# Splitting the negated softmax maxima before their transpose, and noise on a planner's due times

## The chip, the cores and the metric

The kernel runs on one core of one Trainium2 chip. The core has TensorE (matmuls), VectorE, ScalarE and GpSimd (elementwise work), and SyncE, whose queue (SP) issues all data transfers of this kernel. The metric is the device time of one execution in microseconds (us); of several runs the median is given.

## What is computed

The reference is a transformer block of two parts, each behind a modulated layer norm and added to its input through a gate. The first part is causal attention in four segments of 512 tokens with a compressive memory; the second mixes tokens with a two-layer MLP.

```python
for s in range(4):                         # 32 heads of 32 channels
    logits = einsum("bhqd,bhkd->bhqk", qs, ks) * scale + mask
    a_dot = einsum("bhqk,bhkd->bhqd", softmax(logits), vs)
    a_mem = (phi(qs) @ M) / (phi(qs) @ z + 1e-6)
    o = g * a_mem + (1 - g) * a_dot
    M, z = M + phi(ks).T @ vs, z + phi(ks).sum(l)
x = x + ga * (o @ wo)
u = gelu(einsum("bsd,sf->bdf", layernorm(h2), w1) + b1)
x = x + gb * (einsum("bdf,fs->bds", u, w2) + b2).transpose()
```

What matters here is the softmax: the maximum of each query's logits is subtracted before the exponential.

## The kernel before, in words

**Number format.** The large matmuls run on float32 values rounded to a shorter format (fp32r), so each operand is split into a high part and the remainder, a low part, and three products are summed (high x high, high x low, low x high). `split` (lines 103 to 110) does this with a ScalarE copy and a VectorE subtraction.

**Attention.** The 32 items of work are (pass, group of four heads, segment): 8 groups of heads x 4 segments, in two passes of two segments. An item is called t, its heads h = 0..3, and n = 4t + h counts heads over all. For each item `project` computes keys and values (L176) and queries (L184) on TensorE, and `stack` (L342 to L344) sends the high and low parts of queries and keys of each head into a stacked tile sk of 98 partitions: 96 for the three products, and two more, 96 and 97, that hold 1 on the key side and the negated maximum, high and low part, on the query side. One matmul over 98 partitions thus gives logits with the maximum already subtracted.

**Maxima.** `maxima(t, h)` multiplies queries by keys over the first 96 partitions (L448), one block of 128 queries at a time, into the banks sx, sy and sz of PSUM (two banks under the tag s1), and VectorE adds the mask and reduces each block to a maximum per query (L449), written to a column of mx. A pair of heads shares one mx tile of 128 queries x 8 columns (2 heads x 4 blocks). After the second head of a pair: TensorE transposes mx to 8 x 128 (L455) into the PSUM bank with the tag ms, ScalarE copies it with the sign turned and rounded (nt0, L457), VectorE computes the remainder (nt1, L458), and SP issues four transfers (L462) of four rows of nt, 2 KB each, into partition 96 or 97 of sk, in the order first head high, first head low, second head high, second head low. There are 64 such pairs.

**Scores and values.** `scores(t, h)` follows three heads later (LEADS): logits from all 98 partitions (L472, L475, L478, L479), exponentials on ScalarE (L473, L476, L480), the causal edge and the split of the result on GpSimd and ScalarE (L483, L485, L487), and then `values` (L501) multiplies by the values. L472 is the first instruction that needs the negated maxima in sk.

**After attention.** An output projection (L691) with layer norms follows, then the MLP as block products (L790) with results added by VectorE (L797). These stages stream large weight transfers through SP.

**What sets the order.** The program is first written down in the order of the loops; then `set_order` plans it. `Order.forward` is a list scheduler: it gives every instruction a cost (`cost`, `transfer`), walks time forward, and on each engine picks, among the ready instructions, the one with the smallest key. `Order.backward` does the same from the end and returns a due time for each, which is the next key. This is done three times (PASSES), and the order of the last forward pass is imposed on each engine's queue, SP's too. Every queue runs in order: an instruction that waits holds up all behind it. In the plan a transfer of at most 4096 bytes takes 580 ns to issue, and lands 130 ns after the transfers issued before it.

Of the kernel before, what the change touches and what calls it, by code (L numbers as in the profile page):

```python
# [4 lines left out]

# [4 lines left out]
F32 = mybir.dt.float32  # L10
F32R = mybir.dt.float32r
F16 = mybir.dt.float16
BF16 = mybir.dt.bfloat16
AF = mybir.ActivationFunctionType
ALU = mybir.AluOpType
# [5 lines left out]
P = 128  # L21
# [17 lines left out]
HB = 3  # L39
WO0 = 65  # L40
WOS = 6
TILES = (3, 4, 5, 6, 0, 1, 8, 2, 9, 10, 11, 7, 12, 13, 14, 15)


def attention_and_mlp(ctx, tc, x, wq, wkv, wo, beta, w1, b1, w2, b2, c, wm_a, wm_b, out):
    nc = tc.nc
    V, A, G, T, SY = nc.vector, nc.scalar, nc.gpsimd, nc.tensor, nc.sync
# [17 lines left out]
    a = par.__enter__()  # L65
# [11 lines left out]
    def bank(tag, bufs, name):  # L77
        return psum.tile([P, 512], F32, tag=tag, bufs=bufs, name=name)

    A.preload_act_table_set("natural_log_exp_and_others")  # L80
    ident = top.tile([P, P], F32, name="ident")
# [182 lines left out]
    for i in range(2):  # L264
        ps = bank("pj", 2, f"scps{i}")
# [47 lines left out]
    b = late.__enter__()  # L313
# [124 lines left out]
    def maxima(t, h):  # L438
        d = st[t]
        if h % 2 == 0:  # L440
            d["mx"] = b.tile([P, 2, 4], F32, tag="mx", bufs=2, name=f"mx{t}_{h}")
        mx = d["mx"]
        q, k = d["sk", h][0:96, 0], d["sk", h][0:96, 1]
        x = bank("s1", 2, f"sx_{t}_{h}")
        y = bank("s1", 2, f"sy_{t}_{h}")
        z = bank("s1", 2, f"sz_{t}_{h}")
        for i, o in ((0, x[:, 0:128]), (2, x[:, 128:512]), (1, y[:, 0:256]), (3, z)):
            T.matmul(o, q[:, 128 * i:128 * i + 128], k[:, 0:128 * i + 128], start=True, stop=True)  # L448
            V.tensor_tensor_reduce(  # L449
                o, o, mask[:, 384 - 128 * i:], 1.0, -3.0e38, op0=ALU.add, op1=ALU.max,  # L450
                accum_out=mx[:, h % 2, i:i + 1])
        if h % 2 == 0:
            return
        ps = bank("ms", 1, f"nmps{t}_{h}")
        T.transpose(ps[0:8, 0:128], mx.rearrange("p a b -> p (a b)"), ident)  # L455
        nt = [b.tile([8, P], F32R, tag=f"nt{i}", bufs=2, name=f"nt{i}_{t}_{h}") for i in range(2)]
        A.activation(nt[0], ps[0:8, 0:128], AF.Copy, scale=-1.0)  # L457
        V.scalar_tensor_tensor(nt[1], ps[0:8, 0:128], -1.0, nt[0].bitcast(F32), op0=ALU.mult, op1=ALU.subtract)  # L458
        for hh in range(2):
            sk = d["sk", h - 1 + hh]  # L460
            for part in range(2):
                SY.dma_start(sk[96 + part:97 + part, 0].bitcast(F32).rearrange("p (b n) -> p b n", n=128),  # L462
                             nt[part][4 * hh:4 * hh + 4].bitcast(F32))

    def scores(t, h):
        d = st[t]
# [126 lines left out]
    for g in range(2, NG):  # L593
        n = 8 * g - 13
# [5 lines left out]
    for j in range(32):  # L600
        n = ML0 + MLS * j
        later(n, lambda j=j: mod_fetch(j), n + 2, lambda r, j=j: mod_late(j, r))
    plan(WO0 - 3, lambda: spread(gaw, 0))
    for i in range(8):
        n = WO0 + WOS * i
        later(n, lambda i=i: wo_fetch(i), n + 2, lambda r, i=i: wo_split(i, r))

    for n in range(-LEADS, 4 * NI + VL):
# [4 lines left out]
        if 0 <= m + 4 < 4 * NI:  # L613
            t = (m + 4) // 4
# [8 lines left out]
        if 4 * NI - 5 <= m < 4 * NI + 3:  # L623
            i = m - 4 * NI + 5
# [107 lines left out]

    for tt in TILES:
        rest = out_proj(tt)
# [132 lines left out]
    for u, (ph, g) in enumerate(units):  # L867
# [59 lines left out]
        t = tp.tile([P, 3, 512], F32, tag="tu", bufs=1, name=f"tu{g}")  # L927
# [26 lines left out]
                             acc[g][:, 2 * m:2 * m + 2].rearrange("p a n -> p (a n)"))  # L954


ISSUED, LANDED, READ = 900.0, 500.0, 500.0
BACKLOG, BULK = 1000.0, 200000
LATE = 1000.0
LATEB = 3000.0  # L960
HOLD = 1000.0
EARLY = 60000.0
LINK0, SPREAD, QUICK = 2000.0, 45000.0, 1.0
EAGER = 200.0
WD, WA = 250.0, 100.0
SOON = 30000.0
WAIT = {"DVE": WD, "Activation": WA}
STAY = 3000.0
SLACK = 1.06
DMA_SPREAD = 7000.0  # L970
DONE = 11.0
LINK = 1
COLD = 20000.0
SPARE = 40000.0
MINT = 5
AVOID = 0.0
FREED = 60.0
WAKE = {"PE": 150.0, "DVE": 23.0, "Activation": 23.0, "Pool": 70.0, "SP": 60.0}
RIGHT = ("top", "st2", "late2", "b3", "wr", "s1", "cw")
PASSES = 3  # L980


def space(t):
    return str(t.space)
# [51 lines left out]
def tiled(x):  # L1036
    return [a for a in (*x.outs, *x.ins) if hasattr(a, "bass_ap")]


def cost(x):  # L1040


    e, op = x.engine.name, x.opcode
    n = max((math.prod(s[1] for s in list(v.ap)[1:]) for v in (*x.outs, *x.ins) if hasattr(v, "ap")), default=1)
    aps = tiled(x)
    if e == "PE":
        m = x.ins[0]
        c, dt = math.prod(s[1] for s in list(m.ap)[1:]), m.dtype
        if dt == F32:
            held = 223 if c in (132, 1) else 111  # L1050
        elif dt == F32R:
            held = max(63, c / 2.25 + (20 if aps[0].bass_ap.tensor.name[0] == "a" else 4))
        else:
            held = c / 2.26
        return held, held + 170, False
    if op == "DMACopy":
        return transfer(x)[0], 0, False
    psum = any(hasattr(v, "bass_ap") and space(v.bass_ap.tensor) == "PSUM" for v in x.ins)
    ins = sum(hasattr(v, "bass_ap") for v in x.ins)
    shared = False  # L1060
    if e == "DVE":
        if op == "ISA":
            return 135 + 1.05 * n, 220 + 1.05 * n, False
        if op == "TensorTensor":
            d = 145 + 1.055 * n
        elif op == "TensorScalarPtr":
            d = 155 if n < 64 else 120 + 1.1 * n
        else:
            d = {"TensorCopy": 820, "BNStats": 680, "TensorReduce": 554}.get(op, 195)
        shared = n >= 256 and ins > 1 and not psum  # L1070
    elif e == "Activation":
        if op == "TensorCopy":
            d = 185 + 0.76 * n if psum else 200 + 0.825 * n
        else:
            d = 250 + 0.85 * n + (150 if ins > 2 else 0) if n > 8 else 250
    elif op == "TensorTensor":
        d = {512: 1500, 640: 1454, 1024: 2900}.get(n, 520)
    elif op == "TensorScalarAffineSelect":
        d = 180 + n
    else:  # L1080
        d = 110 + 0.95 * n
    d *= SLACK
    return d - 85, d, shared


class Order:
# [192 lines left out]
    def forward(self, key):  # L1279
# [21 lines left out]
        def add(i):  # L1301
# [10 lines left out]
            x = self.X[i]  # L1312
            more = HOLD if self.side(x) and ready[i] > EARLY else 0.0
            if self.spread(i):
# [12 lines left out]
        while len(seq) < n:  # L1327
            t, e, i = self.pick(free, heap, future, key)
            soon = WAIT.get(e, 0.0) if t < SOON else 0.0
            if soon and future[e] and future[e][0][0] <= t + soon:  # L1330
                near = [(key[j], r, j) for r, j in future[e] if r <= t + soon]
                k, r, j = min(near)
                if k < key[i] - EAGER and r < t + self.C[i][0]:
                    heapq.heappush(heap[e], (key[i], i))
# [49 lines left out]
            for s in strong[i]:  # L1384
                done(s, t if E[s] == e == "PE" else fin[i] + WAKE.get(E[s], 30.0))
            for s in weak[i]:
                done(s, t + 1)
            for tl in tiles_of[i]:
                left[tl] -= 1
                freed[tl] = max(freed[tl], fin[i] + FREED)  # L1390
                if not left[tl]:
# [21 lines left out]
    def backward(self, start, fin, seq):  # L1413
# [9 lines left out]
        for old, i in self.took:  # L1423
            for u in self.users[old]:
                if u != i:
                    before[i][u] = max(fin[u] - start[u] + FREED, before[i].get(u, 0))
        for i in range(n):
            for d in before[i]:
                open_[d] += 1
        due = [max(s, d - SPARE) for s, d in zip(start, self.due(before, start, fin, seq))]  # L1430
        free, heap, future = defaultdict(float), defaultdict(list), defaultdict(list)
# [4 lines left out]
        for _ in range(n):  # L1436
            t, e, i = self.pick(free, heap, future, key)
            z = max(t, ready[i])
            late[i], free[e] = -z, z + (max(transfer(self.X[i])[:2]) if LINK and e == "SP" else self.C[i][0])
            for d, lag in before[i].items():  # L1440
# [4 lines left out]
        return late  # L1445


def set_order(nc, tc):

    o = Order(list(nc.cur_bb.bb.instructions))  # L1450
    start, fin, seq = o.forward(range(len(o.X)))
    for _ in range(PASSES):
        start, fin, seq = o.forward(o.backward(start, fin, seq))
    prev = {}
    behind = mybir.DependencyInfo(mybir.DependencyClass.NoSync, mybir.DependencyReason.DATA)
    for i in seq:
        x, e = o.X[i], o.E[i]
        if e in WAKE:
            if e in prev:
                tc.add_manual_dep(x, prev[e], behind, reason="order")  # L1460
            prev[e] = x.name
    return max(fin)
# [38 lines left out]
```

## Time and profile before

| what | us |
|---|---|
| median of three runs | 2209.34 |
| runs | 2207.14, 2209.35, 2209.34 |
| the profiled execution's own time | 2212.39 |
| its span, first to last instruction | 2210.6 |
| TensorE busy | 2170.2 |
| VectorE busy | 1728.2 |
| ScalarE busy | 1099.7 |
| GpSimd busy | 715.1 |

In the profile PE is TensorE's matmuls, PEld its weight loads, DVE VectorE, ACT ScalarE, POOL GpSimd, SP the queue of SyncE, and SPq and the like the queues that issue. L462 is line 462 of the kernel. `sk<-nt` is an operation that writes tile sk from tile nt. Idle time of an engine is put down to what ended it. A busy TensorE isn't one at its peak, since matmuls are pipelined: the idle time counts as lost, the busy time says little. PEclk is the clock that was granted to TensorE, as a share of full speed.

### The profile page before, as it was taken

To read this page: it belongs to the slowest core of one execution; us is meant where nothing else is said; L and a number is where in the kernel's file an instruction comes from. 1 tells how busy PE (TensorE), PEld (TensorE's weight loads), DVE (VectorE), ACT (ScalarE), POOL (GpSimd) and SP (SyncE) were. 2 spreads that over 40 slices of the span, in tenths; PEclk is the share of its full clock that TensorE was granted. 3 is DMA by queue.
4 is the path that set the end of the run, shared out by engine and by line. 5 is a ranking of instruction groups with operands and counts; after the bars stand their busy time and mean duration, and the time that the engine had idled before them with its cause. 6 is when DMAs were issued, how large, how long until landed. Compare 5 with 4: busy or idle time off the path is not lost.

```text
span 2210.6 us, 38316 instructions
## 1 busy us (share of the span) xinstructions
PE 2170.2 (98%) x13760; PEld 1882.7 (85%) x13760; DVE 1728.2 (78%) x3817; ACT 1099.7 (50%) x2008; POOL 715.1 (32%) x829
## 2 busy tenths in 40 slices
PE   8999999999999999999999999999999999999999
PEld 7899998989898999978878888888888888888887
DVE  8787776867787755678997555898889787878787
ACT  6687787566665766562434333533334242424232
POOL 1476676476776756570001000043221000000000
PEclk9999999999999999999999999999999999999999
DMA  9667666796677643674467555775549241414144
GB/s 384 193 192 215 174 213 190 240 292 201 194 227 237 184 131 101 173 243 164 138 238 274 193 200 191 276 272 202 200 175 335 92 157 58 147 54 148 58 124 152
DMA packets 174769, 421.74 MB, mean 191 GB/s; under 512 B 17356, under 2 KB 71668, under 8 KB 165620
## 3 DMA queue, kind: packets, MB, share of 16 engines
q1 hardware_dynamic: 174580, 419.30, 58.2%
q8 instruction: 109, 1.79, 0.3%
q14 instruction: 80, 0.66, 0.1%
HBM read 242.00 MB, written 126.37 MB: 167 GB/s over the span
## 4 chain that ended last, share of the span: by engine, by line
PE 85%; DVE 5%; DMA 4%; ACT 2%; POOL 2%; issue 1%; SPq 0%; DVEq 0%; ACTq 0%; POOLq 0%
PE mx L790 47%; PE nps L176 12%; PE po L691 6%; PE qps L184 6%; PE pv L501 4%; POOL ph L487 1%; PE a L472 1%; PE sx L448 1%; PE sz L448 1%; PE up L430 1%; PE rd L420 1%; DVE wm L286 1%; PE a L475 1%; DMA rawv<-in_wkv_dram 1%; DMA sk<-nt 1%
## 5 line engine op out<-in xcount | busy, mean ns | idle before, releaser
L790 PE MATMUL mx<-bU,sp 128*128 128x512 f32 x2352 | 533.7, 389 | 0.8 <-DVE bU L110 0.8
L790 PEld LDWEIGHTS mx<-bU,sp 128*128 128x128 f32 x2352 | 441.3, 188 | 93.0 <-DVE bU L110 1.2
L107 ACT CAST sp<-wr 128x384 fp32r<-128x384 f32 (+2 forms) x408 | 218.4, 545 | 468.8 <-PE mx L790 382.9
L176 PE MATMUL nps<-wv,h 128*128 128x256 f32 x3072 | 440.3, 283 | 1.9 <-DVE r L373 1.4
L790 PE MATMUL mx<-bA,sp 128*128 128x512 f32 x1764 | 433.5, 390 | 1.7 <-ACT sp L107 0.9
L487 POOL TENSOR_TENSOR ph<-p,ph 128x640 f16<-128x640 f32 x256 | 385.6, 1523 | 104.6 <-ACT ph L485 104.2
L176 PEld LDWEIGHTS nps<-wv,h 128*128 128x128 f32 x3072 | 402.0, 189 | 8.4 <-DVE r L373 1.6
L790 PEld LDWEIGHTS mx<-bA,sp 128*128 128x128 f32 x1764 | 330.6, 188 | 72.9 <-ACT sp L107 1.9
L110 DVE TENSOR_TENSOR sp<-wr,sp 128x384 fp32r<-128x384 f32 (+2 forms) x408 | 257.3, 639 | 60.4 <-ACT sp L107 60.0
L797 DVE TENSOR_TENSOR ac<-mx,ac 128x512 f32<-128x512 f32 x280 | 190.5, 687 | 94.8 <-PE mx L790 93.9
L184 PE MATMUL qps<-h,wq 128*128 128x512 f32 x768 | 199.6, 403 | 0.0
L485 ACT CAST ph<-p 128x1280 f16<-128x1280 f32 x128 | 161.3, 1260 | 48.3 <-POOL p L483 47.9
L691 PE MATMUL po<-wo,ots 128*128 128x512 f32 x768 | 181.7, 391 | 0.5 <-DVE x L694 0.3
L691 PEld LDWEIGHTS po<-wo,ots 128*128 128x128 f32 x768 | 143.1, 188 | 29.9 <-DVE x L694 0.9
L184 PEld LDWEIGHTS qps<-h,wq 128*128 128x128 f32 x768 | 141.3, 191 | 29.1 <-issue 0.3
L790 PE MATMUL mx<-bB,sp 128*128 128x512 f32 x588 | 165.7, 389 | 0.0
L483 POOL TENSOR_SCALAR_AFFINE_SELECT p<-p 128x256 f32<-128x256 f32 x256 | 118.0, 471 | 134.5 <-ACT p L476 95.7
L449 DVE CUSTOM_DVE_ANT_0 sx<-sx,mask 128x128 f32<-128x128 f32 (+1 forms) x256 | 110.6, 433 | 62.6 <-PE sx L448 60.4
L662 POOL TENSOR_TENSOR tu<-cc 128x512 f32<-128x512 f32 x14 | 20.0, 1426 | 399.2 <-DVE cc L926 372.2
L790 PEld LDWEIGHTS mx<-bB,sp 128*128 128x128 f32 x588 | 110.4, 188 | 22.9
L501 PE MATMUL pv<-vp,ph 128*128 128x97 bf16 (+1 forms) x2560 | 118.3, 201 | 0.1
L501 PEld LDWEIGHTS <-ph 128*128 128x128 f16 x2560 | 108.1, 98 | 5.8 <-issue 1.2
(184 smaller groups left out, 3246.4 us busy)
## 6 DMA issues: line engine op xcount, KB each, us to landing
sk<-sg SPq DMA_DIRECT2D x384, 128.0 KB
wr<-in_w_dram SPq DMA_DIRECT2D x28, 1024.0 KB
wr<-in_w_dram SPq DMA_DIRECT2D x32, 768.0 KB
bstu<-ucd SPq DMA_DIRECT2D x28, 768.0 KB
wv<-wsp SPq DMA_DIRECT2D x36, 512.0 KB
wsp<-wv SPq DMA_DIRECT2D x32, 512.0 KB
rawm<-in_wm_b_dram SPq DMA_DIRECT2D x32, 512.0 KB
pcd<-cc SPq DMA_DIRECT2D x14, 1024.0 KB
```

The source lines that it names most:

```text
L107: A.copy(hi, src)
L110: lo_eng.tensor_tensor(lo, src, hi.bitcast(F32), op=ALU.subtract)
L176: T.matmul(ps[:, aa], h[:, j, 128 * tt:128 * tt + 128], wt[:, i, o:o + 256], start=(n == 0), stop=(n >= 6 * NK - 2), skip_group_check=True)
L184: T.matmul(ps, wt[:, i, o:o + 128], h[:, j], start=(k + n == 0), stop=(3 * k + n == 3 * NK - 1))
L449: V.tensor_tensor_reduce(o, o, mask[:, 384 - 128 * i:], 1.0, -3.0e38, op0=ALU.add, op1=ALU.max, accum_out=mx[:, h % 2, i:i + 1])
L483: G.affine_select(w, w, pattern=[[0, 2], [1, 128]], compare_op=ALU.is_ge, fill=0.0, base=0, channel_multiplier=-1)
L485: A.copy(ph[:, 0], p32)
L487: G.tensor_tensor(ph[:, 1, c], p32[:, c], ph[:, 0, c], op=ALU.subtract)
L501: T.matmul(pv[:, i, 0:w], ph[:, part, o:o + 128], d["vp"][:, j, h, 0:w], start=(n == 0), stop=(n == 19), skip_group_check=True)
L691: T.matmul(ps, os_[:, i, P * ct:P * ct + P], wop[ct, nh][:, j], start=(n == 0), stop=(n == 3 * NK - 1))
L790: T.matmul(ps, ops[q][:, i, P * k:P * k + P], b[:, j], start=(m == 0 and first), stop=(m == 3 * nk - 1), skip_group_check=True)
L797: V.tensor_tensor(d, ps, d, op=ALU.add)
```

## The change

Three things are changed. First, VectorE negates the maxima and takes their high and low parts before the transpose, on the 128 x 8 tile, into a new tile mm of 128 x 16 with four buffers (MM); its columns are ordered by head, then part, then block. TensorE transposes 16 columns at once, ScalarE copies 16 x 128 to one tile nt (three buffers in place of two of each part), and one transfer for each head moves eight rows of nt, 4 KB, into partitions 96 and 97 of sk.

Second, after the last pass of the planner a further forward pass is run, with the same due times plus noise: `nudged` adds a Gaussian number to the due time of every instruction whose planned start lies in a stretch. There are 25 entries of (seed, from, to, width), times in ns of the plan.

Third, many constants of the planner can be read from the environment; their values are as before.

```diff
@@ maxima, after the second head of a pair
+        mm = b.tile([P, 2, 2, 4], F32R, tag="mm", bufs=MM, name=f"mm{t}_{h}")
+        V.tensor_scalar(mm[:, :, 0], mx, -1.0, None, op0=ALU.mult)
+        V.scalar_tensor_tensor(mm[:, :, 1], mx, -1.0, mm[:, :, 0].bitcast(F32), op0=ALU.mult, op1=ALU.subtract)
         ps = bank("ms", 1, f"nmps{t}_{h}")
-        T.transpose(ps[0:8, 0:128], mx.rearrange("p a b -> p (a b)"), ident)
-        nt = [b.tile([8, P], F32R, tag=f"nt{i}", bufs=2, name=f"nt{i}_{t}_{h}") for i in range(2)]
-        A.activation(nt[0], ps[0:8, 0:128], AF.Copy, scale=-1.0)
-        V.scalar_tensor_tensor(nt[1], ps[0:8, 0:128], -1.0, nt[0].bitcast(F32), op0=ALU.mult, op1=ALU.subtract)
+        T.transpose(ps[0:16, 0:128], mm.rearrange("p a c b -> p (a c b)").bitcast(F32), ident)
+        nt = b.tile([16, P], F32R, tag="nt", bufs=3, name=f"nt{t}_{h}")
+        A.copy(nt, ps[0:16, 0:128])
         for hh in range(2):
             sk = d["sk", h - 1 + hh]
-            for part in range(2):
-                SY.dma_start(sk[96 + part:97 + part, 0].bitcast(F32).rearrange("p (b n) -> p b n", n=128),
-                             nt[part][4 * hh:4 * hh + 4].bitcast(F32))
+            SY.dma_start(sk[96:98, 0].bitcast(F32).rearrange("p (b n) -> p b n", n=128),
+                         nt[8 * hh:8 * hh + 8].bitcast(F32))
...
+NUDGES = (
+    (839485, 482000.0, 512000.0, 300.0),
+    (324712, 922000.0, 1022000.0, 100.0),
+    (608137, 521000.0, 551000.0, 300.0),
+    (337605, 0.0, 30000.0, 800.0),
+    (965332, 417000.0, 1517000.0, 100.0),
...
+    (347681, 480000.0, 510000.0, 800.0),
...
+    (684163, 133000.0, 163000.0, 300.0),
...
+)
...
+def nudged(o, key, start, nudges):
+    key = list(key)
+    for seed, lo, hi, width in nudges:
+        rnd = random.Random(seed)
+        for i in range(len(key)):
+            if lo <= start[i] < hi:
+                key[i] += rnd.gauss(0.0, width)
+    return key
...
     start, fin, seq = o.forward(range(len(o.X)))
     for _ in range(PASSES):
-        start, fin, seq = o.forward(o.backward(start, fin, seq))
+        key = o.backward(start, fin, seq)
+        start, fin, seq = o.forward(key)
+    start, fin, seq = o.forward(nudged(o, key, start, NUDGES))
```

Of the 25 stretches, four begin before 200 us, two between 200 and 300, and the other 19 lie from 370 us on, all but one of them ending by 1022 us.

More of the change, by code (lines that the diff above doesn't have):

```diff
@@ L2 @@
 import math
+import random
 from collections import defaultdict
@@ L41 @@
 WOS = 6
+MM = 4
 TILES = (3, 4, 5, 6, 0, 1, 8, 2, 9, 10, 11, 7, 12, 13, 14, 15)
@@ L954, in attention_and_mlp @@
                              acc[g][:, 2 * m:2 * m + 2].rearrange("p a n -> p (a n)"))
+import os
+EV = lambda n, d: type(d)(os.environ.get(n, d))
 ISSUED, LANDED, READ = 900.0, 500.0, 500.0
-BACKLOG, BULK = 1000.0, 200000
-LATE = 1000.0
+BACKLOG, BULK = EV("BACKLOG", 1000.0), 200000
+LATE = EV("LATE", 1000.0)
 LATEB = 3000.0
 HOLD = 1000.0
[L962 to L966, printed above, removed]
+EARLY = EV("EARLY", 60000.0)
+LINK0, SPREAD, QUICK = EV("LINK0", 2000.0), EV("SPREAD", 45000.0), 1.0
+EAGER = EV("EAGER", 200.0)
+WD, WA = EV("WD", 250.0), EV("WA", 100.0)
+SOON = EV("SOON", 30000.0)
 WAIT = {"DVE": WD, "Activation": WA}
-STAY = 3000.0
+STAY = EV("STAY", 3000.0)
 SLACK = 1.06
 DMA_SPREAD = 7000.0
-DONE = 11.0
-LINK = 1
+DONE = EV("DONE", 11.0)
+LINK = EV("LINK", 1)
 COLD = 20000.0
-SPARE = 40000.0
+SPARE = EV("SPARE", 40000.0)
 MINT = 5
 AVOID = 0.0
-FREED = 60.0
-WAKE = {"PE": 150.0, "DVE": 23.0, "Activation": 23.0, "Pool": 70.0, "SP": 60.0}
+FREED = EV("FREED", 60.0)
+WAKE = {"PE": EV("WP", 150.0), "DVE": 23.0, "Activation": 23.0, "Pool": 70.0, "SP": EV("WS", 60.0)}
 RIGHT = ("top", "st2", "late2", "b3", "wr", "s1", "cw")
-PASSES = 3
+NUDGES = (
[4 more added lines that the diff above has]
+    (965332, 417000.0, 1517000.0, 100.0),
+    (781737, 833000.0, 933000.0, 100.0),
+    (929601, 783000.0, 813000.0, 800.0),
+    (705508, 676000.0, 706000.0, 300.0),
+    (882468, 168000.0, 268000.0, 100.0),
+    (566630, 374000.0, 404000.0, 300.0),
+    (347681, 480000.0, 510000.0, 800.0),
+    (910697, 791000.0, 821000.0, 100.0),
+    (866938, 611000.0, 711000.0, 800.0),
+    (789657, 398000.0, 498000.0, 100.0),
+    (755375, 694000.0, 794000.0, 800.0),
+    (180523, 822000.0, 852000.0, 800.0),
+    (491307, 882000.0, 912000.0, 100.0),
+    (179681, 703000.0, 803000.0, 300.0),
+    (901513, 718000.0, 748000.0, 100.0),
+    (684163, 133000.0, 163000.0, 300.0),
+    (535242, 250000.0, 280000.0, 100.0),
+    (27380, 277000.0, 577000.0, 100.0),
+    (297005, 760000.0, 860000.0, 800.0),
+    (142077, 140000.0, 170000.0, 100.0),
+    (495461, 800000.0, 830000.0, 300.0),
+)
+PASSES = EV("PASSES", 3)
 def space(t):
@@ L1066, in cost @@
         elif op == "TensorScalarPtr":
-            d = 155 if n < 64 else 120 + 1.1 * n
+            d = EV("SMALL", 155) if n < 64 else 120 + 1.1 * n
         else:
```

## The prediction

> **What bounds the kernel now.** I read the page first, then busy time by stage, then the waits of TensorE, then the instructions that end its gaps.
>
> ```profile
> span 2210.6 us, 38316 instructions
> PE 2170.2 (98%) x13760; PEld 1882.7 (85%) x13760; DVE 1728.2 (78%) x3817; ACT 1099.7 (50%) x2008; POOL 715.1 (32%) x829
> ```
>
> TensorE is the bound: it is idle for 2210.6 - 2170.2 = 40.4 us. So an edit elsewhere pays only through a gap on TensorE. The stages say where the gaps lie (columns: stretch, busy us of each engine, granted clock, DMA share, GB/s):
>
> ```profile
> 0.00:50.00 50.00, 41.90 (x260) 37.33 (x261) 45.01 (x100) 28.61 (x47) 8.90 (x33) 1.00 0.97 385
> 50.00:980.00 930.00, 904.66 (x8066) 835.54 (x8065) 677.71 (x2049) 626.65 (x1153) 603.19 (x726) 0.99 0.67 201
> 980.00:1180.00 200.00, 199.12 (x927) 163.62 (x926) 186.81 (x368) 78.42 (x149) 13.71 (x13) 1.00 0.56 190
> 1180.00:2210.60 1030.60, 1024.55 (x4513) 846.23 (x4511) 818.69 (x1301) 366.00 (x662) 89.33 (x59) 1.00 0.49 173
> ```
>
> The attention stage, 50 to 980 us, holds 930.00 - 904.66 = 25.3 us of idle and the only clock below 1.00. All that the change touches in the arithmetic is in this stage. TensorE's waits of the whole span, largest first where lines are left out:
>
> ```profile
> PE a L472 <- DMA sk<-nt: 9.4, 6, 3.4
> PE a L478 <- ACT p L473: 6.4, 10, 2.0
> ...
> PE sz L448 <- DVE mx L449: 1.3, 3, 0.8
> PE sx L448 <- DVE mx L449: 1.2, 2, 0.7
> PE sx L448 <- DMA sk<-sg: 1.2, 3, 0.6
> ```
>
> The largest wait is the one for the negated maxima (nt) to land in the stacked operand (sk): six gaps, 9.4 us. These are the matmuls that end them, with two other gaps for comparison (the bracket is the idle time):
>
> ```profile
> 61.46 0.74 PE L176 MATMUL nps<-wv,h 128*128 128x256 f32 x4 [1.37 <-DVE r L373]
> 80.92 0.47 PE L472 MATMUL a<-sk 98*128 98x512 f32 x1 [1.53 <-DMA sk<-nt]
> 359.83 0.47 PE L472 MATMUL a<-sk 98*128 98x512 f32 x1 [0.82 <-DMA sk<-nt]
> 374.72 0.47 PE L472 MATMUL a<-sk 98*128 98x512 f32 x1 [3.39 <-DMA sk<-nt]
> 593.44 0.52 PE L478 MATMUL a<-sk 98*128 98x256 f32 x1 [2.01 <-ACT p L473]
> 671.27 0.47 PE L472 MATMUL a<-sk 98*128 98x512 f32 x1 [1.69 <-DMA sk<-nt]
> 952.65 0.47 PE L472 MATMUL a<-sk 98*128 98x512 f32 x1 [1.49 <-DMA sk<-nt]
> 961.35 0.47 PE L472 MATMUL a<-sk 98*128 98x512 f32 x1 [0.48 <-DMA sk<-nt]
> ```
>
> A gap costs more than itself. The granted clock just behind some of them (after the stretch: its length, TensorE busy, clock):
>
> ```profile
> 61.00:66.00 5.00, 4.54 (x38) 1.00 0.95 281
> 81.00:86.00 5.00, 5.00 (x18) 0.66 0.40 158
> 374.00:379.00 5.00, 4.28 (x35) 0.66 0.53 190
> 593.00:598.00 5.00, 4.56 (x37) 0.66 1.03 275
> 671.00:676.00 5.00, 4.73 (x14) 0.66 0.75 247
> 952.00:957.00 5.00, 4.35 (x39) 1.00 1.02 402
> ```
>
> The gaps of 1.53, 3.39, 2.01 and 1.69 us are each followed by a clock of 0.66 over 5 us: 0.34 x 5 = 1.7 us of work lost. Those of 1.37 and 1.49 us are not. So in this trace the line lies near 1.5 us, and three of four dips belong to the nt wait.
>
> **The change, part by part.** The old chain of a pair of heads: transpose of the maxima (L455), copy with sign by ScalarE (L457), rest by VectorE (L458), four transfers of 2 KB (L462). Engine rows of count, and min/median/max in ns; the last two are the nearest small VectorE operations on 128x8:
>
> ```profile
> L462 SPq DMA_DIRECT2D sk<-nt x256: 572/578/1069, 76.3 to 963.7; - x128
> L457 ACT ACTIVATE nt<-nmps x64: 247/262/268, 76.0 to 959.0; 8x128 fp32r<-8x128 f32 x64
> L458 DVE SCALAR_TENSOR_TENSOR nt<-nmps,nt x64: 262/274/280, 76.3 to 959.3; 8x128 fp32r<-8x128 f32 x64
> L455 PE MATMUL nmps<-ident,mx x64: 269/271/418, 75.7 to 958.7; 128*8 128x128 f32 x64
> L422 DVE TENSOR_SCALAR rdd<-rd x48: 146/160/178, 98.1 to 940.9; 128x8 f32<-128x8 f32 x48
> L423 DVE RECIPROCAL rdd<-rdd x48: 189/198/205, 98.3 to 941.1; 128x8 f32<-128x8 f32 x48
> ```
>
> *VectorE.* Two 128x8 operations replace one of 8x128. Their price isn't in the trace; I bound a pair by 2 x 146 = 0.29 us below and 2 x 280 = 0.56 us above (the old 8x128 form), and take 0.160 + 0.198 = 0.36, the rows of their shape. Less the 0.274 removed, that is +0.085 us a pair (bounds +0.02 to +0.29), 64 x 0.085 = 5.4 us on an engine with 677.71 busy of 930: hidden unless it stands ahead of a maxima reduction that TensorE waits for (first rival).
>
> *TensorE.* The transpose still streams 128 columns; only the stationary side grows from 8 to 16. I take 271 ns as before and no gain or loss. It now waits 0.36 us longer for VectorE, and every matmul queued behind it waits with it; the planner puts other matmuls ahead of it, as it does now.
>
> *ScalarE.* One copy of 16x128 for 8x128 with a scale: same columns, 262 ns, nothing.
>
> *Buffers.* mx is free once VectorE has split it, and the one "ms" bank is free after ScalarE's copy rather than after VectorE's: 0.27 us earlier for the next user. No wait of TensorE on that bank is among the large ones, so nothing.
>
> *Transfers.* 128 of 256 go. At 578 ns each that is 74 us of SP's issue time over 930. What it gives TensorE stands in the SP queue around four of the gaps (start, us, how many) and in the chain that ended last:
>
> ```profile
> 76.32 2.60 SPq L462 DMA_DIRECT2D sk<-nt  x4
> 354.57 0.58 SPq L462 DMA_DIRECT2D sk<-nt  x1
> 357.42 1.95 SPq L462 DMA_DIRECT2D sk<-nt  x3
> 368.33 3.03 SPq L462 DMA_DIRECT2D sk<-nt  x4
> 664.78 3.06 SPq L462 DMA_DIRECT2D sk<-nt  x4
> ```
>
> ```profile
> 77.08 3.70 DMA sk<-nt
> 357.42 2.28 DMA sk<-nt
> 369.50 5.08 DMA sk<-nt
> 665.53 5.61 DMA sk<-nt
> ```
>
> Each time the second of the four, the first head's low part, is what the matmul waits for. Its issue starts 77.08 - 76.32 = 0.76, 357.42 - 354.57 = 2.85, 369.50 - 368.33 = 1.17 and 665.53 - 664.78 = 0.75 us after the first. With one transfer a head, that step is gone. The chain ahead of it grows by 0.36 and loses 0.274, so +0.09, and the flight of 2.3 to 5.6 us stays. That leaves cuts of 0.7, 2.8, 1.1 and 0.7 us. For the other two gaps I take the least, 0.7. Capped by each gap: 0.7 + 0.82 + 1.1 + 0.7 + 0.7 + 0.48 = 4.5 of the 9.4 us (bounds: 0 if flight grows as much, 9.4 if the planner moves the chain clear).
>
> *Clock.* The gap of 1.53 falls to 0.8 and that of 1.69 to 1.0, below the 1.49 that left the clock alone: two dips, 2 x 1.7 = 3.4 us. The gap of 3.39 falls to 2.3 and keeps its dip. [...]
>
> *Other transfers.* The 1.2 us of waits on sk<-sg stand behind the same queue; each is at most 0.6 us, one issue. I credit half, 0.6 (bounds 0 to 1.2).
>
> *New order.* The noise moves due times by 0.1 to 0.8 us (standard deviations of each entry), in stretches that cover most of 370 to 1020 us of the plan, a few pieces before it, and, weakly, the mixer up to 1517. It changes no instruction, only which goes first; a cost in the plan that changes re-deals every queue too. What it can win is bounded by the 25.3 us of idle plus four dips of 1.7: 32 us. What it can lose has no bound in the trace; the largest gap there, with its dip, is 3.39 + 1.7 = 5.1, and I take two such, 10 us. With no row that favours a sign I take 0. The stages after 980 us have 0.9 and 6.0 us of idle and no clock loss, so it matters little there.
>
> Sum: 4.5 + 3.4 + 0.6 = 8.5 us less. The profiled execution took 2212.4 us, 1.8 more than its span and 3.1 more than the median of the runs, 2209.3. Taken from the median: 2200.8 us.
>
> **Rivals.** *VectorE ahead of the banks (slower).* The two new operations stand right behind a pair's last reduction, so the next pair's first reduction, and the bank it frees for TensorE, comes 0.36 us later, while the removed one stood elsewhere. The price is 0.36 a pair, at most 64 x 0.36 = 23 us. For it: TensorE already waits for these reductions (1.3 + 1.2 us). Against: that is five waits among 64 pairs, and VectorE is busy 73% of the stage. It decides from about 24 pairs on the path (24 x 0.36 = 8.6, what the sum gains). At 40 pairs: 14.4 - 8.5 = +6, 2215 us.
>
> *Nothing gained.* The nt gaps close and another wait opens at the same places: the second group, on ScalarE's exponentials (6.4 us, ten times), is the next step of the same head. If it takes back the cut and the dips stay, 2209 us, give or take 4. For it: ScalarE and GpSimd are both above 600 us busy there. Against: those gaps are mostly below 1 us and at other places.
>
> *The order does more.* Half of what is left of idle and dips goes with the new order: (25.3 - 4.5 - 0.6)/2 + 3.4/2 = 12 us more, 2189 us. For: the gaps are few and each has its own accident in a queue, such as the three transfers put between the first and second nt transfer at 354.57. Against: noise has no aim.
>
> [...]
>
> **How the numbers follow.** Forecast case 0.47 (its own range 2196 to 2205), the order does more 0.19, nothing gained 0.17, slower flight 0.06, VectorE ahead of the banks and other slower orders 0.11. What a measurement of this kernel can tell from no change is about 0.2%, 4.4 us. Faster: 0.47 + 0.19 = 0.66; same: 0.17 + 0.06 = 0.23; slower 0.11. The range runs from the larger gain, 2188, to the upper end of no change, 2213; it leaves out most of the slower case and a tail below.
>
> **What would show it.** In the new profile: 128 nt transfers in place of 256; TensorE's wait on sk<-nt at 5 us or less; idle time in 50 to 980 us near 20 us; two or fewer stretches at half clock; waits of TensorE on the maxima reductions still some 3 us. A step is wrong if the transfers' flight is longer, if the wait on the reductions grows past 5 us, or if idle falls at places that have nothing to do with nt: then the order did it. The forecast is wrong if the idle time stays at 25 us.

## The result, and the profile after

The changed kernel takes 2228.37 us (median of four runs, 2226.37 to 2229.26) against 2209.09 for the kernel before (four runs, 2207.14 to 2209.35). The ratio is 1.0086, interval 1.0074 to 1.0098: it is slower by 19 us. Forecast were 2200.8 us, 2188 to 2213, and 0.66 for faster. The profiled execution took 2228.47 us.

The top of the page of the changed kernel:

```profile
span 2225.7 us, 38145 instructions
PE 2170.1 (97%) x13760; PEld 1881.6 (85%) x13760; DVE 1763.4 (79%) x3881; ACT 1101.6 (49%) x2008; POOL 710.0 (32%) x829
```

TensorE is as busy as before, 2170.1 against 2170.2 us. Its idle time grew from 40.4 to 55.6 us, and that is the whole of the 15.1 us by which the two profiled spans differ (2225.7 and 2210.6). One engine has clearly more work: VectorE, 1763.4 against 1728.2. The same stretches as in the prediction say where the idle time lies:

```profile
0.00:50.00 50.00, 38.71 (x243) 34.33 (x244) 44.99 (x99) 27.09 (x44) 7.39 (x30) 1.00 0.97 379
50.00:980.00 930.00, 893.09 (x7981) 824.72 (x7980) 699.69 (x2092) 621.74 (x1142) 587.16 (x718) 1.00 0.67 198
980.00:1180.00 200.00, 197.46 (x954) 161.94 (x953) 183.75 (x363) 81.38 (x153) 24.09 (x23) 1.00 0.54 177
1180.00:2225.70 1045.70, 1040.80 (x4587) 860.58 (x4585) 834.96 (x1329) 371.40 (x673) 91.39 (x60) 1.00 0.49 175
```

In the attention stage the idle time is 930.00 - 893.09 = 36.9 us; it was 25.3 and was forecast near 20. The start, 0 to 50 us, has 11.3 in place of 8.1; a gap of 2.9 us there ends with ScalarE's split of a weight (wv, in the list below), ahead of the first new operation, so it belongs to the new order. From 1180 us on it is 4.9, not more than before. TensorE's waits in the changed kernel, of the whole span:

```profile
PE nmps L460 <- DVE mm L458: 8.7, 10, 1.6
PE a L475 <- DMA sk<-nt: 5.4, 6, 2.2
PE a L481 <- ACT p L476: 5.2, 8, 1.5
...
PE sx L450 <- DVE mx L451: 2.9, 6, 1.7
PE nps L178 <- ACT wv L109: 2.9, 1, 2.9
...
PE nmps L460 <- DVE am L426: 2.4, 3, 1.0
...
PE sz L450 <- DVE mx L451: 1.8, 3, 0.8
...
PE sx L450 <- DMA sk<-sg: 1.0, 1, 1.0
```

The wait that the change aimed at did shrink, from 9.4 to 5.4 us. The first line is new: ten times TensorE stands at the transpose (now L460) until the split on VectorE (L457 and L458) is done, 8.7 us; three more times it stands there behind an earlier VectorE operation, 2.4 us. That is 11.1 us lost at VectorE for 4.0 won at the transfers. These are the new chain's instructions (count, then min/median/max in ns):

```profile
L457 DVE TENSOR_SCALAR mm<-mx x64: 120/178/1293, 75.6 to 973.3; 128x8 fp32r<-128x8 f32 x64
L458 DVE SCALAR_TENSOR_TENSOR mm<-mx,mm x64: 151/296/1368, 76.0 to 973.9; 128x8 fp32r<-128x8 f32 x64
L465 SPq DMA_DIRECT2D sk<-nt x128: 610/648/1260, 78.1 to 976.2; - x128
L462 ACT CAST nt<-nmps x64: 234/252/257, 77.1 to 975.2; 16x128 fp32r<-16x128 f32 x64
L460 PE MATMUL nmps<-ident,mm x64: 269/272/416, 76.8 to 974.9; 128*16 128x128 f32 x64
```

The number of transfers, the copy and the transpose are as forecast. An issue takes 0.648 us in place of 0.578, so that SP issues for 128 x 0.648 = 83 us in place of 256 x 0.578 = 148. The first two rows are not as forecast: the fastest take 0.12 and 0.15 us, the slowest nine to eleven times that, for the same 128 x 8 tile. A median hides this; the groups by line give the sums (busy us, mean ns):

```profile
L458 DVE SCALAR_TENSOR_TENSOR mm<-mx,mm 128x8 fp32r<-128x8 f32 x64 | 33.9, 529 | 0.7
L457 DVE TENSOR_SCALAR mm<-mx 128x8 fp32r<-128x8 f32 x64 | 25.2, 393 | 0.4
```

A pair costs 0.92 us, not 0.36: 59.1 us in all, less the 17.5 of the removed operation, is 41.6 us more. What a slow one looks like, on the timelines of VectorE, GpSimd and TensorE (start, us):

```profile
450.16 0.80 DVE L457 TENSOR_SCALAR mm<-mx 128x8 fp32r<-128x8 f32 x1
451.00 1.31 DVE L458 SCALAR_TENSOR_TENSOR mm<-mx,mm 128x8 fp32r<-128x8 f32 x1
...
449.52 2.76 POOL L490 TENSOR_TENSOR ph<-p,ph 128x640 f16<-128x640 f32 x2
...
452.36 0.28 PE L460 MATMUL nmps<-ident,mm 128*16 128x128 f32 x1 [1.50 <-DVE mm L458]
```

GpSimd computes the low part of the probabilities (L490), two operations that end at 449.52 + 2.76 = 452.28 us. VectorE's L458 ends at 451.00 + 1.31 = 452.31, just behind, and only then can TensorE start its transpose, after 1.50 us of idling. This holds throughout: of the 128 operations 66 take more than 190 ns, and each of these 66 ends 16 to 33 ns behind the end of some GpSimd operation. Those that meet no GpSimd operation (24 of the 64 of L457, 23 of L458) take 120 to 172 ns.

### The profile page after: what moved, and what is told of

It reads as the page before. It is cut to its first block, busy times and chain, and to the rows that moved or that the text cites. A ratio compares the mean times of both kernels' runs of the same rounds, so it can differ in the third digit from the quotient of the medians.

```text
span 2225.7 us, 38145 instructions
## 1 busy us (share of the span) xinstructions
PE 2170.1 (97%) x13760; PEld 1881.6 (85%) x13760; DVE 1763.4 (79%) x3881; ACT 1101.6 (49%) x2008; POOL 710.0 (32%) x829
## 4 chain that ended last, share of the span: by engine, by line
PE 79%; DVE 10%; DMA 4%; ACT 3%; issue 2%; POOL 1%; SPq 1%; DVEq 0%; POOLq 0%; ACTq 0%
PE mx L793 47%; PE nps L178 11%; PE po L694 6%; PE qps L186 4%; PE pv L504 3%; PE sx L450 1%; DVE mm L458 1%; PE a L475 1%; PE sz L450 1%; DMA sk<-nt 1%; PE up L432 1%; DVE sg L112 1%; DVE rawm L533 1%; DVE wm L288 1%; PE rd L422 1%
## 5 line engine op out<-in xcount | busy, mean ns | idle before, releaser
L178 PE MATMUL nps<-wv,h 128*128 128x256 f32 x3072 | 450.8, 285 | 3.3 <-ACT wv L109 2.9
L178 PEld LDWEIGHTS nps<-wv,h 128*128 128x128 f32 x3072 | 409.0, 190 | 10.7 <-ACT wv L109 3.3
L490 POOL TENSOR_TENSOR ph<-p,ph 128x640 f16<-128x640 f32 x256 | 380.8, 1506 | 106.7 <-ACT ph L488 104.6
L800 DVE TENSOR_TENSOR cc<-mx,cc 128x512 f32<-128x512 f32 x140 | 95.4, 684 | 23.6 <-PE mx L793 21.7
```

The source lines that it names most:

```text
L178: T.matmul(ps[:, aa], h[:, j, 128 * tt:128 * tt + 128], wt[:, i, o:o + 256], start=(n == 0), stop=(n >= 6 * NK - 2), skip_group_check=True)
L490: G.tensor_tensor(ph[:, 1, c], p32[:, c], ph[:, 0, c], op=ALU.subtract)
L800: V.tensor_tensor(d, ps, d, op=ALU.add)
```

## The experiments

The theory with which they began: the new chain costs the time, by VectorE's two operations. The rivals: the noise does it (the random order is simply a worse one), or the one larger transfer does it, or the transpose's wait does it and not VectorE's time as such. All runs first, in the order of the ratio; each ratio stands against the kernel before on the same chip, and "draw" is one setting of the random numbers.

| kernel | maxima split by | noise | median, us | ratio | interval |
|---|---|---|---|---|---|
| e9 | old chain | other draw | 2212.40 | 1.0016 | 1.0006 to 1.0025 |
| e2 | old chain | the change's | 2213.65 | 1.0024 | 1.0015 to 1.0033 |
| e12 | GpSimd | none | 2214.08 | 1.0029 | 1.0015 to 1.0044 |
| e10 | old chain | third draw | 2216.83 | 1.0035 | 1.0021 to 1.0049 |
| e6 | VectorE, planner told | none | 2218.96 | 1.0054 | 1.0038 to 1.0071 |
| e7 | VectorE, four transfers | none | 2220.61 | 1.0055 | 1.0038 to 1.0073 |
| e5 | ScalarE and VectorE from PSUM | none | 2219.04 | 1.0059 | 1.0036 to 1.0082 |
| e14 | GpSimd | the change's | 2219.82 | 1.0059 | 1.0041 to 1.0076 |
| e11 | VectorE, told, four transfers | none | 2219.92 | 1.0061 | 1.0039 to 1.0084 |
| e3 | VectorE | other draw | 2223.45 | 1.0067 | 1.0052 to 1.0082 |
| e15 | VectorE, planner told | the change's | 2225.35 | 1.0086 | 1.0067 to 1.0105 |
| after | VectorE | the change's | 2228.37 | 1.0086 | 1.0074 to 1.0098 |
| e1 | VectorE | none | 2226.86 | 1.0089 | 1.0068 to 1.0110 |
| e13 | old chain, idle copies on VectorE | none | 2234.03 | 1.0123 | 1.0102 to 1.0145 |
| e4 | as e5, one more constant tile | none | 2249.90 | 1.0188 | 1.0171 to 1.0205 |

One kernel more, e8, leaves work out: its time says nothing, and only its durations are read.

### Chain or noise

The new chain without the noise (e1), the noise on the old chain (e2), and the change with other random numbers (e3):

```diff
 e1:
-NUDGES = (
...
+NUDGES = ()
 e2: maxima as in the kernel before, planner and NUDGES as in the change
 e3:
-        rnd = random.Random(seed)
+        rnd = random.Random(seed + 1)
```

> The changed kernel with an empty list of noise entries: the new split and the single transfers alone. Theory A (the two VectorE operations on SBUF tiles are slowed while GpSimd works, and TensorE's transpose waits for them): 2220 to 2230 us, the two operations at some 390 and 530 ns mean, TensorE's wait on mm again 7 us or more. Theory B (the noise spoils the order): 2200 to 2210 us.

> The kernel before with the further noisy pass and its 25 entries, the old split and four transfers. Theory A: within 6 us of the kernel before, 2203 to 2215 us. Theory B: 2218 us or more.

> The changed kernel with every seed raised by one, the same stretches and widths. Theory A: within 6 us of the changed kernel, 2222 to 2234 us, with mm as slow as before. Theory B (this draw is a bad one): a different draw gives another time, as likely near 2210 us as above 2228.

The chain without the noise is as slow as the change: 1.0089 beside 1.0086. The noise put on top changes nothing that can be told in the change's own draw, and another draw differs from it by 0.2%, with intervals that overlap. On the old chain the noise costs 0.24%. So the noise is not what makes the change slow. Two more draws on the old chain (seed + 1 and seed + 2 in the line above) show what a draw is worth there:

> The kernel before with the noisy pass, every seed raised by one: a second draw beside e2. Theory D (the order of the kernel before is a good draw, and any new one costs something): 2211 to 2220 us, TensorE's idle time ahead of the mixer 36 us or more against 33.9. Theory E (the order makes no difference beyond 4 us; the new chain costs all the rest): 2205 to 2213 us.

> As e9 with every seed raised by two, a third draw. Theory D: 2211 to 2220 us. Theory E: 2205 to 2213 us.

Both are slower than the kernel before, as e2 is: 0.16, 0.24 and 0.35%. Three draws of three lose a little, and they differ among themselves by about 0.2%. The profiles don't show this loss as idle time of TensorE (38.2 and 37.1 us in e9 and e10, 40.4 in the kernel before), so where it lies is open. A difference of a few us between two kernels that were planned anew is therefore no evidence of a cause, which bears on several of the readings below.

But the two chains stay apart: the three orders of the new one (e1, after, e3) lie at 1.0067 to 1.0089, all above the three new orders of the old one at 1.0016 to 1.0035. The means are 0.81 and 0.25%. So by an estimate from these six some 0.56%, or 12 us, is the new chain; the rest of the 19 us is about what the new orders of the old chain lost.

### Who holds the two operations

In e8 GpSimd writes zeros in place of the subtraction L490, so that it no longer reads the probabilities there. (The low part of the probabilities is then missing.)

```diff
-            G.tensor_tensor(ph[:, 1, c], p32[:, c], ph[:, 0, c], op=ALU.subtract)
+            G.memset(ph[:, 1, c], 0.0)
```

> e1 with GpSimd's subtraction that forms the low part of the exponentials left out: it fills that part with zeros, so 256 operations that read two tiles become 256 that only write. The low part of the probabilities is missing from the output. Theory A (VectorE's SBUF operations are held while GpSimd reads SBUF): the two mm operations fall from means near 390 and 530 ns to below 250 ns each. If something else stretches them, they stay above 350 ns. The time of this kernel says nothing, since GpSimd has 200 us less to do.

The groups of e1, and behind them those of e8:

```profile
L458 DVE SCALAR_TENSOR_TENSOR mm<-mx,mm 128x8 fp32r<-128x8 f32 x64 | 27.0, 422 | 0.6
L457 DVE TENSOR_SCALAR mm<-mx 128x8 fp32r<-128x8 f32 x64 | 25.9, 404 | 0.3
```

```profile
L457 DVE TENSOR_SCALAR mm<-mx 128x8 fp32r<-128x8 f32 x64 | 28.4, 444 | 0.4
L458 DVE SCALAR_TENSOR_TENSOR mm<-mx,mm 128x8 fp32r<-128x8 f32 x64 | 17.1, 267 | 0.9
```

L458, which has two inputs in SBUF, falls from 422 to 267 ns when GpSimd no longer reads there. L457, with one input, doesn't fall: 444 ns. Below 250 was expected of both; L458 came near it, L457 did not. GpSimd's zeros are also quicker than its subtraction (632 for 1509 ns), so a shorter hold could by itself explain L458. Single operations settle this. Here is one of each beside two operations that write zeros (start, us):

```profile
234.87 1.20 POOL L490 MEMSET ph<- 128x640 f16 x2
235.69 0.41 DVE L457 TENSOR_SCALAR mm<-mx 128x8 fp32r<-128x8 f32 x1
...
597.91 1.24 POOL L490 MEMSET ph<- 128x640 f16 x2
598.87 0.16 DVE L458 SCALAR_TENSOR_TENSOR mm<-mx,mm 128x8 fp32r<-128x8 f32 x1
```

L457 ends at 236.10 us, just behind the zeros' 236.07. L458 runs its 0.16 us in the midst of them. So it is throughout e8: of the 34 operations of L457 over 190 ns, 24 end just behind an operation that only writes; of the 13 of L458, none does, and all end just behind one that reads. So in e8 L457 is held by operations that only write too, and L458 is not; what sets the two apart no run here shows. Not every operation with one input in SBUF is held: the reciprocal L423 of the kernel before took 189 to 205 ns in all 48 cases, and GpSimd was at work in 32 of them.

The other side is a split that reads PSUM. In e5 ScalarE writes each maximum to both its columns, TensorE transposes all 16, ScalarE rounds them, and VectorE takes the rounded value off what stands in PSUM, high rows with a factor of 0 and low rows with 1:

```diff
-        V.tensor_scalar(mm[:, :, 0], mx, -1.0, None, op0=ALU.mult)
-        V.scalar_tensor_tensor(mm[:, :, 1], mx, -1.0, mm[:, :, 0].bitcast(F32), op0=ALU.mult, op1=ALU.subtract)
+        A.copy(mm, mx.unsqueeze(2).to_broadcast([P, 2, 2, 4]))
...
-        A.copy(nt, ps[0:16, 0:128])
+        A.copy(hi, ps[0:16, 0:128])
...
+        V.scalar_tensor_tensor(nt, hi.bitcast(F32), low, ps[0:16, 0:128], op0=ALU.mult, op1=ALU.subtract)
```

> No noise. ScalarE doubles the maxima into 16 columns, TensorE transposes 16 at once, ScalarE rounds, and VectorE forms high and low rows in one operation that reads PSUM; one transfer for each head as in the change. No VectorE operation reads only SBUF tiles any more. Theory A: that operation stays near 270 ns, and the time falls to 2200 to 2212 us. Theory B: as e1. If the single transfer itself costs (a longer flight), 2215 us or more under both.

> e4 with its 16 constants kept in a tile that was there as padding, so that every other tile stands where it stood in the kernel before. Theory C (e4 lost its time after attention because one more tile moved the operands, so that a matmul took 233 in place of 227 ns): matmuls of the mixer at 227 ns again, 2205 to 2218 us. If e4's loss belongs to the split, 2240 us or more again.

The two differ only in where the 16 factors `low` lie: a constant tile of its own in e4, a corner of a padding tile that was there already in e5. VectorE's operation in e5, by its tile's rows:

```profile
L468 DVE SCALAR_TENSOR_TENSOR nt<-hi,pad,nmps x64: 318/330/335, 77.6 to 967.0; 16x128 fp32r<-16x128 f32 x64
```

From 318 to 335 ns, never held in 64 times, though GpSimd was at work in 51 of them. So this subtraction, with one input from PSUM, is not held, while L458 of the changed kernel, with both from SBUF, took 151 to 1368 ns. The time of e5 is 1.0059, lower than e1's, but the intervals overlap; it is not at the kernel before, and just above the 2205 to 2218 us that were expected. What remains in it is not settled: its chain has one ScalarE operation more, and its order is a draw of its own. The extra loss of e4 isn't in attention at all, and is told in the last section.

### A wait in the chain, or time on VectorE

In e13 the old chain stays, without noise, and VectorE makes the two operations besides, with nobody reading what they write:

```diff
         if h % 2 == 0:
             return
+        mm = b.tile([P, 2, 2, 4], F32R, tag="mm", bufs=MM, name=f"mm{t}_{h}")
+        V.tensor_scalar(mm[:, :, 0], mx, -1.0, None, op0=ALU.mult)
+        V.scalar_tensor_tensor(mm[:, :, 1], mx, -1.0, mm[:, :, 0].bitcast(F32), op0=ALU.mult, op1=ALU.subtract)
```

> The kernel before, no noise, with the new split's two VectorE operations added for each pair and their result unused: the old chain makes the negated maxima as before. Theory F (the held operations cost as VectorE time, wherever they stand): 2214 to 2224 us. Theory G (they cost because TensorE's transpose and the transfers wait for them): 2206 to 2214 us, the level of the old chain's other draws.

It is the slowest but for e4: 1.0123, or 2234 us, above both expectations (the higher was 2214 to 2224). The two operations cost it 59 us of VectorE (28.6 + 30.3, its groups):

```profile
L458 DVE SCALAR_TENSOR_TENSOR mm<-mx,mm 128x8 fp32r<-128x8 f32 x64 | 30.3, 474 | 0.7
L457 DVE TENSOR_SCALAR mm<-mx 128x8 fp32r<-128x8 f32 x64 | 28.6, 447 | 0.3
```

TensorE waits on nothing that they write, and yet it idles 52.1 us in place of 40.4. (Its busy time grew too, by 8.0 us, which isn't explained; nor is it shown why e13 loses more than the change does.) Its waits in e13:

```profile
PE a L483 <- ACT p L478: 9.0, 12, 2.0
...
PE sx L450 <- DVE mx L451: 4.4, 6, 1.4
...
PE up L432 <- DVE am L426: 3.6, 5, 1.7
...
PE sz L450 <- DVE mx L451: 2.1, 3, 1.5
PE nmps L460 <- DVE am L426: 1.9, 2, 1.1
PE up L432 <- DVE pv L509: 1.7, 1, 1.7
```

The largest single wait is for ScalarE's exponentials, 9.0 us where it was 6.4. The sum by engine tells more. These are all of TensorE's gaps, added up by the engine that ended them (us; several kernels of one kind as least to most):

| kernels | VectorE | ScalarE | transfers |
|---|---|---|---|
| old chain: before, e2, e9, e10 | 5.3 to 13.1 | 11.6 to 15.1 | 7.2 to 11.5 |
| split on VectorE: after, e1, e3, e6, e7, e11, e15 | 18.6 to 27.7 | 13.6 to 19.5 | 0.8 to 6.4 |
| old chain with idle copies: e13 | 25.0 | 16.0 | 5.2 |
| split on GpSimd: e12, e14 | 8.5, 14.3 | 19.1, 16.5 | 7.8, 4.0 |
| split that reads PSUM: e4, e5 | 13.6, 11.8 | 20.6, 21.4 | 4.0, 6.3 |

Every whole kernel with the two operations on VectorE loses 18.6 us or more at VectorE's outputs, e13 among them, and none without them more than 14.3; no draw crosses this line. (In e8, where L458 is mostly free, it is 16.2.) So the operations cost as time on VectorE, and the place of the wait is only where that time comes out. The rival, that the loss needs the transpose's wait, falls twice: in e13 no transpose waits for them, and in e15 (below) the transpose waits 1.5 us for them and the time is still 1.0086. An engine that is busy for 73% of a stage was not one with room to spare.

That predicts that a split off VectorE is cheaper. In e12, otherwise e1, GpSimd makes it, without a sign, and ScalarE's copy turns the sign; the planner is told 265 ns for each of GpSimd's two operations:

```diff
-        V.tensor_scalar(mm[:, :, 0], mx, -1.0, None, op0=ALU.mult)
-        V.scalar_tensor_tensor(mm[:, :, 1], mx, -1.0, mm[:, :, 0].bitcast(F32), op0=ALU.mult, op1=ALU.subtract)
+        G.tensor_copy(mm[:, :, 0], mx)
+        G.tensor_tensor(mm[:, :, 1], mx, mm[:, :, 0].bitcast(F32), op=ALU.subtract)
...
-        A.copy(nt, ps[0:16, 0:128])
+        A.activation(nt, ps[0:16, 0:128], AF.Copy, scale=-1.0)
```

> [...] If VectorE's held operations are the loss of the new chain: 2209 to 2219 us, VectorE's busy time some 70 us lower than in e1. If a longer chain is the loss whatever engine it is on (GpSimd's queue holds operations of 1.5 us): 2222 us or more.

> e12 with the 25 noise entries of the change: a second draw of the order for the split on GpSimd. If that chain is level with the old one: 2208 to 2217 us, as the old chain's draws (2209 to 2217). If e12 was a lucky draw: 2219 us or more.

e14 is e12 with the change's noise. The page of e12:

```profile
PE 2166.8 (98%) x13760; PEld 1878.9 (85%) x13760; DVE 1703.0 (77%) x3753; ACT 1098.3 (50%) x2008; POOL 732.7 (33%) x957
```

VectorE falls to 1703.0 us, 60.4 below the changed kernel, and the loss with it: 1.0029 against 1.0089 of e1, and 1.0059 against 1.0086 with noise. Of all kernels with the new chain e12 is the best, and it is within the draws of the old chain. Its second draw e14 is not: 2219.82 us is what was expected if e12 was a lucky draw. By the medians the split is cheaper off VectorE in both pairs (with noise the intervals just touch), but it isn't shown to be level with the old chain. No kernel tried here beats the one before, although e12 has the single transfers and less work on VectorE.

### The plan and the transfers

In e6 the planner is told what the two operations cost; in e7 the new chain issues two transfers of 2 KB for each head in place of one of 4 KB; e11 does both; e15 is e6 with the change's noise.

```diff
 e6, in cost():
+    if aps and aps[0].bass_ap.tensor.name.startswith("mm") and n == 8:
+        d = 500 if ins > 1 else 370
 e7:
-            SY.dma_start(sk[96:98, 0]..., nt[8 * hh:8 * hh + 8]...)
+            for part in range(2):
+                SY.dma_start(sk[96 + part:97 + part, 0]..., nt[8 * hh + 4 * part:8 * hh + 4 * part + 4]...)
```

> e1 (no noise) with the two operations on mm costed in the plan at 1.06 x 370 and 1.06 x 500 ns in place of 1.06 x 155 each, near their measured means of 390 and 530. If the loss comes from a plan that puts the transpose too close behind them: 2210 to 2219 us, TensorE's wait on mm below 3 us. If it comes from VectorE's own time and from the spread of the durations: 2220 to 2230 us.

> e1 with two transfers of 2 KB for each head in place of one of 4 KB, all else the same. If the single transfer gains what was forecast (some 5 us of waits and a dip or two): 2231 to 2238 us, TensorE's wait on sk<-nt back near 9 us. If transfers don't matter: within 5 us of e1, 2222 to 2232 us.

> e6 and e7 together: the plan told the measured cost of the two operations, and two transfers for each head. If telling the plan (8 us) and four transfers (6 us) are two gains: 2211 to 2215 us. If four transfers were only another draw of the order: 2216 to 2223 us.

> e6 with the 25 noise entries of the change: a second draw for the plan that is told the measured cost. If telling the plan is worth 5 us or more over the draws: 2214 to 2221 us. If e6 was a lucky draw: 2223 to 2229 us, as the new chain's three draws.

With a cost near the measured means in the plan (e6) TensorE's wait at the transpose for the split falls from 6.1 us in e1 to 0.6, and the time is 8 us below e1. But with the noise on top (e15) it is 1.0086 again, as the change itself. A gain that another draw takes back is not shown to be the plan's. Four transfers for a pair are 6 us faster than two without the told cost (e7 beside e1) and 1 us slower with it (e11 beside e6): neither form shows an advantage, and e7 lies below both of its expectations. Nor does TensorE wait longer for nt with four: 3.0 us in e7 and 2.4 in e11, beside 0.4 in e1 and 1.2 in e6. So the halved number of transfers, for which the chain was rebuilt, is worth nothing that can be measured here, though it shortens SP's queue by 65 us.

## Why the prediction was wrong

**The step that failed** is the VectorE term: "take 0.160 + 0.198 = 0.36, the rows of their shape", hence "+0.085 us a pair" and "5.4 us on an engine with 677.71 busy of 930: hidden". It failed twice. The price was 0.92 us a pair, above even the upper bound of 0.56, so the term was 41.6 us and not 5.4. And it was not hidden: e13 puts the same work beside the old chain and loses 1.2%. The rows for the price had the right shape and the wrong operands: L422 reads PSUM (146 to 178 ns), and L423, a reciprocal with one input in SBUF, isn't held beside GpSimd (189 to 205 ns). The bound above came from a row that reads PSUM as well (the old L458, 262 to 280 ns), so it was no bound. The trace of the kernel before had rows of the right kind, larger operations with both inputs in SBUF:

```profile
L401 DVE SCALAR_TENSOR_TENSOR pk<-k,rk x24: 670/734/1919, 58.0 to 912.1; 128x512 f32<-128x512 f32 x24
L408 DVE TENSOR_TENSOR vp<-r,vp x32: 670/688/1948, 63.9 to 930.7; 128x512 bf16<-128x512 f32 x32
```

The 17 of L408 that start with no GpSimd operation under way take 670 to 697 ns. The other 15 take up to 1948, and each of those over 700 ends 542 to 551 ns behind the end of a GpSimd operation. The maximum beside the minimum was the warning.

**The rival that came nearest** is *VectorE ahead of the banks*. Its engine was right; its price, 0.36 a pair, was too small, and its place too narrow: TensorE's waits on the reductions grew (sx from 1.2 to 2.9, sz from 1.3 to 1.8), but the larger part came out at the transpose. The text had an argument that the transpose's wait would be covered, "the planner puts other matmuls ahead of it": it does, by a plan that takes the split to be short.

**The new order** was taken as 0 "with no row that favours a sign". On top of the new chain that was about right (1.0089 without, 1.0086 with). On the old chain three draws lost 0.16 to 0.35%, so by the estimate above some 5 us of the miss lie here. A reason that could have been seen ahead is that the order before already was one whose gaps were small, so a random other one is more likely to be worse; this is argued, not shown.

**What held.** ScalarE's copy (252 ns for 262) and the transpose (272 for 271), and 128 transfers. Two more numbers came out by luck. TensorE's wait on sk<-nt is 5.4 us for a forecast 4.9, but it is 5.8 to 7.2 us in the draws of the old chain and 0.4 to 4.2 in the other kernels with the split on VectorE, so its size goes with the order. The dips of the clock are two in the attention stage where there were four, but both stand behind new gaps (1.67 and 2.22 us, below), while the one behind 3.39 us that was to stay is gone. And the 3.4 us that they should give do not show: up to the last stage TensorE is as busy as before (before, then after; the last stage begins at 1135 and 1151 us):

```profile
0.00:1135.00 1135.00, 1101.40 (x9056) 1000.43 (x9056) 865.35 (x2437) 711.84 (x1307) 624.45 (x769) 0.99 0.67 206
```

```profile
0.00:1151.00 1151.00, 1101.30 (x9056) 998.84 (x9056) 900.67 (x2501) 713.98 (x1307) 618.65 (x769) 1.00 0.66 203
```

The idle time ahead of that stage is 33.6 us before and 49.7 after, 16.1 more, against 15.1 by which the two spans differ. A slower flight, to which the chances gave 0.06, no run shows. The flights are 1.78 to 6.37 us in the four that stand in the changed kernel's last chain, where they were 2.28 to 5.61; four of each can't tell whether they are longer:

```profile
78.14 1.78 DMA sk<-nt
...
960.49 6.37 DMA sk<-nt
```

**The line near 1.5 us** for the clock held only roughly. In the changed kernel two gaps of 1.50 us and one each of 1.55 and 1.58 have a full clock behind them, those of 1.67 and 2.22 have 0.66:

```profile
653.89 0.27 PE L460 MATMUL nmps<-ident,mm 128*16 128x128 f32 x1 [1.55 <-DVE mm L458]
...
717.44 0.45 PE L450 MATMUL sx<-sk 96*128 96x384 f32 x1 [1.67 <-DVE mx L451]
```

```profile
653.00:658.00 5.00, 4.11 (x40) 1.00 0.45 166
719.00:724.00 5.00, 4.92 (x40) 0.66 1.04 215
```

Before, 1.53 was enough for a dip and here 1.55 was not, so it isn't a fixed length. In the first 50 us longer gaps left the clock at 1.00 as well: 4.6 and 2.5 us before, 4.6, 2.7 and 2.9 after. The prediction's list of gaps left these out.

**What stays open.** Why e5, e12 and e14 still lose 0.3 to 0.6% with VectorE no busier than in the kernel before: a longer chain or the draw. Their gaps at ScalarE's outputs are the larger ones, 16.5 to 21.4 us against 11.6 to 15.1 in the old chain (the table above), which no run explains. Three draws of the old chain span 0.16 to 0.35%, so runs of this number can't tell. No run has the two operations on VectorE without the hold, so its share of the loss is not shown; at the 0.16 us that one takes away from GpSimd, 128 of them would be busy for 21 of the 59 us.

## What to carry to other kernels

Price an operation by a row with the same operands in the same memories and beside the same neighbours, not only of the same shape, and look at its maximum beside its median: a small VectorE operation with both inputs in SBUF took up to 1.37 us beside GpSimd and 0.16 away from it. An engine at 73% of a stage that feeds the bound engine in many small steps has no slack to be taken for granted; put the same work beside the old chain, unread, and see what it costs. Where a planner's order is re-dealt, measure several deals before a few tenths of a per cent are given to a cause.

## What the runs showed of the hardware that was not expected

With a constant tile of 16 partitions by 4 bytes of its own (e4) the last stage was slower than without it (e5). These are the largest matmul group of that stage in e5 and in e4:

```profile
L799 PE MATMUL mx<-bU,sp 128*128 128x512 f32 x2352 | 533.5, 389 | 0.0
```

```profile
L799 PE MATMUL mx<-bU,sp 128*128 128x512 f32 x2352 | 548.9, 395 | 0.0
```

The matmuls are the same, 2352 of the same form, and take 395 ns in place of 389; from start to start it is 233 in place of 227 ns. e4 takes 2249.90 us and e5 2219.04. The two kernels differ in the tile that holds the factors; that the further tile moved others to new places is the author's estimate. A third group of that stage has the same tile sp and another partner, and its median stays at 389 ns in e4 (its mean is 391, in e5 389):

```profile
L799 PE MATMUL mx<-bB,sp x588: 387/389/398, 1144.2 to 1688.0; 128*128 128x512 f32 x196
```

So it isn't sp by itself. That a new place of the other operand is the reason is a guess, and no run here moved it alone.
